# Fused attention and MLP block: weighted sums of two steps joined into one burst at 24 of 128 steps

## The chip, the cores and the metric

The kernel runs on one core of a Trainium2 chip. The metric is the device time in microseconds of one execution. It stood at 1092.6 us before the change (median of three runs, 1092.5 to 1093.32).

## The reference

The input x has 2048 tokens of width 448. The block adds three things: x itself, an attention and an MLP, both of the layer-normalized x.

```python
xn = layernorm(x)
q = (xn @ wq) in 16 heads of 28;  k = xn @ wk;  v = xn @ wv      # one k and v for all heads
p = softmax(q k^T * 28 ** -0.5);  o = p v
y = layernorm(xn)
out = x + o @ wo + gelu(y @ w1 + b1) @ w2 + b2                   # hidden width 1792
```

The layer norm has no weights. All is float32.

## The kernel before

**Stages.** The 2048 tokens lie as 16 tiles of 128, four tiles to a chunk of 512. Until about 475 us the kernel normalizes x, makes q, k and v, and runs the MLP. After that comes the attention stage, which this change touches; all its order is written out by hand, and each engine works through its own list in that order.

**Units and steps.** A *unit* is a chunk of 512 queries and a group of four heads: 16 units. A unit takes eight *steps*, each of two key tiles of 128: 128 steps, numbered n = 0 to 127, with n = 8u + i for step i of unit u. In units 1 to 15 (`TURNED`) three heads are computed in the step; the weights of the fourth head were computed earlier with queries on the partitions, stored in DRAM (`td`), and come back as `half` tiles, which VectorE transposes.

**What a step issues.** A string in `ORDERS` gives the order of a step, one letter an action; `ORDERS[u in TURNED][n % 2]` picks it.

- `s`: one score matmul of 128 keys x 512 queries (L871), and ScalarE's exp of it into half of a *pair* buffer (L872). Six a step, eight in unit 0.
- `m`: one matmul for the row maxima of later units (L521), and VectorE's maximum of it (L522). At most three in an even step and five in an odd one; a running quota stops them at step 117.
- `t`: one matmul of the fourth heads to come (L555), and VectorE's scaled copy with its maximum (L556); every fourth one ends a row block and frees two exps. In even steps, until the list is empty at step 94.
- `x`: one such exp over 1024 columns on ScalarE (L573), if one is free; each second one issues four stores to `td` on SP's queue.
- `T`: VectorE's transposition of the fourth head's weights for both key tiles of the step (L854), into one pair buffer.
- `n`: the next piece of a finished unit's normalization. `o`: the next piece of an output projection: 12 matmuls (L752 to L754) into one bank and VectorE's addition (L756), in four steps after every fourth unit, and with nine matmuls near the end. `e`: once a unit, the maxima of the next unit are set into its queries.
- `P`: the *burst*. `pv` multiplies the four heads' weights of one key tile by v, each head in its own 32 columns of the array, and adds into the bank `po` (L840); a float32 matmul is two records in the trace, so one key tile is eight records. The burst at the end of step n takes the two key tiles of step n - 1.

**Buffers.** PSUM has eight banks: one is `po`, and seven (`ring`) serve `s`, `m`, `t`, `e` and `o` alike. A matmul that needs a bank waits until an earlier user of one has been read by ScalarE or VectorE. There are `PAIRS` = 9 pair buffers; a step needs four of them (three for six scores, one for the transposition), each until `pv` has read both its halves. A `half` buffer holds four steps' worth of the fourth head; there are three. At the start of every step one part of the next unit's `half` is loaded; before the load VectorE writes one element of it (L723), which takes over the wait for the buffer.

Of the kernel before, what the change touches and what calls it, by code (L numbers as in the profile page):

```python
# [9 lines left out]
F32 = mybir.dt.float32  # L10
F32R = mybir.dt.float32r
# [5 lines left out]
P = 128  # L17
S, D, H, DH, F = 2048, 448, 16, 28, 1792
NT = S // P
CT = 4  # L20
NCH = NT // CT
CW = CT * P
NG = H // 4
NF = F // P
EPS = 1e-5
SCALE = DH ** -0.5
BURST = 2
PAIRS = 9
MLP_MAX = 18
ORDERS = (("nsmsmsnomssmstmssxmP", "nsmsmsemssmsomssnxmP"), ("nmsstTmsosnmssP", "nmsmssxmeosTmsnsmP"))  # L30
TURNED = tuple(range(1, 16))
RAWS = 2
GELU = 0.044715, 0.7978845608028654
LEAD = 11
NH = 8
HD = D // 2

# [2 lines left out]
def block_kernel(ctx, tc, x, wq, wk, wv, wo, w1, b1, w2, b2, out):  # L40
# [4 lines left out]
    def f(t):  # L45
        return t.bitcast(F32)
# [8 lines left out]
    def heads_of(u):  # L55
        return 3 if u in TURNED else 4
# [56 lines left out]
    def mtile(shape):  # L113
        return mp.tile(shape, F32, name="m")
# [97 lines left out]
    def bn_end(c, k0=0, n=CT):  # L212
        for k in range(k0, k0 + n):
            dve.bn_aggr(lnp[:, CT * c + k, :], sts[c][:, k, :])
        ts = slice(CT * c + k0, CT * c + k0 + n)
        r = rstd(lnr[:, ts], lnp[:, ts, 1], n)
        next(r)
        yield
        next(r)
        dve.scalar_tensor_tensor(lnb[:, ts], lnp[:, ts, 0], -1.0, lnr[:, ts], op0=ALU.mult, op1=ALU.mult)  # L220
        yield
# [9 lines left out]
    def norm_both():  # L231
        dve.tensor_mul(lnq, lnp[:, :, 1], lnr)
        dve.tensor_mul(lnq, lnq, lnr)
        r = rstd(lnq, lnq, NT)
        next(r)
        yield
        next(r)
        dve.tensor_mul(lnq, lnq, lnr)
        dve.scalar_tensor_tensor(lnqb, lnp[:, :, 0], -1.0, lnq, op0=ALU.mult, op1=ALU.mult)
        act.activation(warm, one, AF.Tanh)  # L240
        yield
# [61 lines left out]
    def norm_gen(c, bank):  # L303
        center, turn = norm_parts(c, True, False, bank)
        for k in range(CT + 1):
            if k > 0:
                turn(k - 1)
            yield
            if k < CT:
                center(k)  # L310
            yield
# [85 lines left out]
    def spin(n, t=None):  # L397
        for _ in range(n):
            pe.matmul(idle if t is None else t, ident, ident, start=True, stop=True)  # L399
# [9 lines left out]
    for c, at in ((2, ((0, 1), (0, 2), (0, 2), (0, 3))), (3, ((1, 0), (1, 1), (1, 2), (1, 3)))):  # L409
        for k in range(CT):  # L410
            later(*at[k], lambda t=CT * c + k: bn(t))
        g = bn_end(c)
        for k in range(2):
            later(c - 1, 0, lambda g=g: next(g), True)
    g = norm_both()
# [13 lines left out]
    qss, ots = {}, {}  # L429
# [16 lines left out]
    for c in range(NCH):  # L446
        center, turn = norm_parts((c + 1) % NCH, c + 1 == NCH, bank=lambda shape: (qbank, mtile)[next(turns) % 2](shape))
        for i in range(4):
# [7 lines left out]
            if i in ((2, 3) if c == 0 else (1, 3)):  # L456
                n = 2 * c + i // 3
# [216 lines left out]
    for c in range(1, NCH):  # L674
        g = norm_gen(c, lambda shape: php.tile(shape, F32, name="ph"))
# [4 lines left out]
    for n in range(len(mslots) + 2):  # L680
        c, ft = mslots[n] if n < len(mslots) else (NCH, n - len(mslots))
# [28 lines left out]
    att = ctx.enter_context(tc.tile_pool(name="att", bufs=2))  # L710
    mp = ctx.enter_context(tc.tile_pool(name="ring", bufs=7, space=PSUM))
    op = ctx.enter_context(tc.tile_pool(name="op", bufs=1, space=PSUM))

    wor = att.tile([P, NG, D], F32, name="wor", bufs=1)
    halves = {}

    def load_d(u, i):
        assert stored[u] == CT - 1
        h, r = divmod(i, 4)
        if r == 0:  # L720
            halves[u, h] = att.tile([P, 4 * CT, 256], F32, name="half", bufs=3)
        part = halves[u, h][32 * r:32 * r + 32]
        dve.memset(part[0:1, 0, 0:1], 0.0)  # L723
        nc.sync.dma_start(part, td[u][:, r, :, 256 * h:256 * h + 256])

    woh = att.tile([P, NG, D], F32R, name="woh", bufs=1)
    wol = att.tile([P, NG, D], F32R, name="wol", bufs=1)
    pool.memset(wor, 0.0)
# [4 lines left out]
    def prep_wo(g):  # L733
        act.activation(woh[:, g, :], wor[:, g, :], AF.Copy)
        pool.tensor_sub(wol[:, g, :], wor[:, g, :], f(woh[:, g, :]))
# [3 lines left out]
    def load_rows_of(c, tiles):  # L739
        for k in tiles:  # L740
            rows[c, k] = keep.tile([P, D], F32, name="a", bufs=4)
            dve.memset(rows[c, k][0:1, 0:1], 0.0)
            nc.sync.dma_start(rows[c, k], ad[:, CT * c + k, :])

    def o_jobs(c, gs, tiles=range(CT)):
        last = NG - 1 in gs
        for k in tiles:
            po = mtile([P, D])
            ts = slice(k * P, (k + 1) * P)
            for g in gs:  # L750
                oth, otl = ots[c, g]
                pe.matmul(po, oth[:, ts], woh[:, g, :], start=(g == gs[0]), stop=False)  # L752
                pe.matmul(po, oth[:, ts], wol[:, g, :], start=False, stop=False)  # L753
                pe.matmul(po, otl[:, ts], woh[:, g, :], start=False, stop=(g == gs[-1]))  # L754
            a = rows[c, k]
            dve.tensor_add(a, a, po)  # L756
            if last:
                (nc.scalar if k % 2 and c == NCH - 1 else nc.sync).dma_start(ov[:, CT * c + k, :], a)
            yield

    def o_tiles(c, g):
        ots[c, g] = [att.tile([P, CW], F32R, name=n, bufs=5) for n in ("oth", "otl")]
        return ots[c, g]

    def norm_jobs(u, po):
# [36 lines left out]
    def end_jobs(u, po):  # L802
        while side.step() or oside.step():
            pass
        c, g = units[u]
        oth, otl = o_tiles(c, g)
        jobs = o_jobs(c, [g])
        tr, rb, on = att.tile([P, CW], F32, name="tr2", bufs=1), att.tile([P, CW], F32, name="tr", bufs=1), att.tile([P, CW], F32, name="oc", bufs=1)
        rc = att.tile([P, CW // 32], F32, name="rc", bufs=1)
        last = mtile([P, P])  # L810
        spin(9, last)

        def blocks(t, h):
            return t[:, h].rearrange("p (a b) -> p a b", b=32)

        def shares(i):
            h, r = slice(256 * i, 256 * i + 256), slice(8 * i, 8 * i + 8)
            dve.transpose(tr[:, h], po[:, h])
            dve.reciprocal(rc[:, r], blocks(tr, h)[:, :, 0])
            dve.transpose(blocks(rb, h), rc[:, r, None].to_broadcast([P, 8, 32]))  # L820
            dve.tensor_mul(on[:, h], po[:, h], rb[:, h])
            act.activation(oth[:, h], on[:, h], AF.Copy)
            return lambda: dve.tensor_sub(otl[:, h], on[:, h], f(oth[:, h]))

        low = shares(0)
        low()
        low = shares(1)
        next(jobs)
        low()
        for _ in jobs:  # L830
            pass
# [20 lines left out]
    def turn_blocks(u, kt):  # L852
        p = pair_of()
        dve.transpose(p.rearrange("p k (g j) -> p g k j", j=32),  # L854
                      halves[u, kt // 8][:, :, 32 * (kt % 8):32 * (kt % 8) + 64].rearrange("p g (k j) -> p g k j", j=32))
        ps[u, kt, 3], ps[u, kt + 1, 3] = p[:, 0], p[:, 1]

    def pair_of():
        return att.tile([P, 2, CW], F32, name="p", bufs=PAIRS)

# [21 lines left out]
    steps = [(u, kt) for u in range(NU) for kt in range(0, NT, 2)]  # L882
    pvq = [(u, kt) for u in range(NU) for kt in range(NT)]
    total = 4 * CT * len(heads)
    left = total - maxed
    weight = [0 if n >= len(steps) - LEAD else (3, 5)[n % 2] + (u == 0) for n, (u, kt) in enumerate(steps)]
    for n, (u, kt) in enumerate(steps):
        if n == 0:
            loads = pool
        if n == len(steps) - 14:  # L890
            load_rows_of(NCH - 1, range(CT))
        if u + 1 < NU:
            load_d(u + 1, kt // 2)
        if 4 <= n < 4 + NG:
            prep_wo(n - 4)
        if u + 1 < NU and kt < 8:
            load_q(u + 1, (kt // 2,))
        jobs = [(u, kt + k, j) for k in range(2) for j in range(heads_of(u))]
        for what in ORDERS[u in TURNED][n % 2]:
            if what == "s":  # L900
                score(*jobs.pop(0))
            elif what == "m":
                if maxed < total - left + left * sum(weight[:n + 1]) / sum(weight):
                    maxed += mxs.step()
            elif what == "t":
                tq.step()
            elif what == "x":
                turned_exp()
            elif what == "T":
                if u in TURNED:  # L910
                    turn_blocks(u, kt)
            elif what == "e":
                if kt == (6 if u + 2 < NU else 10) and u + 1 < NU:
                    load_max(u + 1)
            elif what == "n":
                side.step()
            elif what == "o":
                if n == len(steps) - 5:
                    oside.add(o_jobs(NCH - 1, range(NG - 1)))
                oside.step()  # L920
            elif what == "P":
                assert not jobs
                for _ in range(BURST if n else 0):
                    pv(*pvq.pop(0))
    while pvq:
        pv(*pvq.pop(0))
# [27 lines left out]
```

## Time and profile before

| | |
|---|---|
| runs | 1092.6, 1092.5, 1093.32 us |
| profiled execution | 1092.67 us, of which 1090.9 us are the span from its first to its last instruction |
| granted TensorE clock | 0.999 |
| TensorE (PE) busy | 1079.5 us, 99% of the span |
| VectorE (DVE) busy | 910.4 us, 83% |
| ScalarE (ACT) busy | 736.4 us, 68% |
| GpSimd (POOL) busy | 562.5 us, 52% |

In rows of instruction groups the columns are line, engine, operation, output and inputs, shapes, count, then the busy time in us and the mean of one in ns, then the engine's idle time before them in us and what ended it. In rows of the timeline they are start in us, length in us, engine, line, operation, output and inputs, shape and count; a bracket holds the idle time before and what ended it. A row of the timeline can stand for several instructions in a row. In a row of a stretch of time they are its bounds, its length, then the busy time of PE, PEld (weight loads), DVE, ACT and POOL with the number of instructions, the granted clock, the share of the DMA engines and GB/s.

### The profile page before, as it was taken

To read this page: it belongs to the slowest core of one execution; us is meant where nothing else is said; L and a number is where in the kernel's file an instruction comes from. 1 tells how busy PE (TensorE), PEld (TensorE's weight loads), DVE (VectorE), ACT (ScalarE), POOL (GpSimd) and SP (SyncE) were. 2 spreads that over 40 slices of the span, in tenths; PEclk is the share of its full clock that TensorE was granted. 3 is DMA by queue.
4 is the path that set the end of the run, shared out by engine and by line. 5 is a ranking of instruction groups with operands and counts; after the bars stand their busy time and mean duration, and the time that the engine had idled before them with its cause. 6 is when DMAs were issued, how large, how long until landed. Compare 5 with 4: busy or idle time off the path is not lost.

```text
span 1090.9 us, 17542 instructions
## 1 busy us (share of the span) xinstructions
PE 1079.5 (99%) x5777; PEld 713.7 (65%) x5777; DVE 910.4 (83%) x1847; ACT 736.4 (68%) x1279; POOL 562.5 (52%) x694
## 2 busy tenths in 40 slices
PE   9999999999999999999999999999999999999998
PEld 8778888888888888865555556555556455555444
DVE  7789889888988998887898997899986889876744
ACT  6675565666666666559777776677775777765783
POOL 6359787778767877854343433433342343243220
PEclk9999999999999999999999999999999999999999
DMA  8774555777877777767977799588797778895720
GB/s 274 214 231 136 154 145 157 194 176 185 217 181 180 183 201 180 214 161 156 200 189 175 183 212 214 141 198 193 183 202 183 175 172 194 203 197 137 183 46 35
DMA packets 140512, 195.15 MB, mean 179 GB/s; under 512 B 17086, under 2 KB 96116, under 8 KB 140420
## 3 DMA queue, kind: packets, MB, share of 16 engines
q1 hardware_dynamic: 127684, 172.11, 63.0%
q0 software_dynamic: 11328, 21.33, 8.9%
q8 instruction: 46, 0.75, 0.3%
q10 hardware_dynamic: 1408, 0.57, 0.2%
q14 instruction: 46, 0.38, 0.1%
HBM read 115.22 MB, written 77.71 MB: 177 GB/s over the span
## 4 chain that ended last, share of the span: by engine, by line
PE 89%; ACT 3%; DVE 3%; DMA 2%; POOL 1%; issue 1%; SPq 0%; DVEq 0%; ACTq 0%; POOLq 0%
PE po L840 22%; PE m L521 17%; PE m L871 17%; PE m L633 10%; PE ph L180 9%; PE m L555 5%; PE qp L180 1%; DMA td<-raw 1%; PE m L752 1%; DVE mx L522 1%; PE m L753 1%; PE m L754 1%; PE ph L185 1%; PE ph L183 1%; ACT raw L573 1%; PE m L399 1%
## 5 line engine op out<-in xcount | busy, mean ns | idle before, releaser
L522 DVE TENSOR_REDUCE mx<-m 128x1 f32<-128x512 f32 x784 | 506.5, 680 | 81.1 <-PE m L521 72.3
L872 ACT ACTIVATE p<-m 128x512 f32<-128x512 f32 x784 | 402.6, 609 | 163.2 <-PE m L871 163.2
L521 PE MATMUL m<-ks,qm 128*128 128x512 f32 x784 | 322.1, 411 | 0.1
L871 PE MATMUL m<-xh,ks 128*128 128x512 f32 x784 | 258.6, 399 | 1.0 <-DVE half L723 1.0
L840 PE MATMUL po<-p,vs 128*32 128x512 f32 x2048 | 246.0, 598 | 0.0
L521 PEld LDWEIGHTS m<-ks,qm 128*128 128x128 f32 x784 | 147.0, 187 | 117.9 <-ACT p L872 34.5
L871 PEld LDWEIGHTS m<-xh,ks 128*128 128x128 f32 x784 | 144.2, 188 | 52.0 <-ACT p L872 15.0
L556 DVE TENSOR_SCALAR_CACHE_REDUCE raw<-m 128x512 f32<-128x512 f32 x240 | 161.1, 689 | 15.2 <-PE m L555 7.0
L854 DVE STREAM_TRANSPOSE p<-half 128x1024 f32<-128x1024 f32 x120 | 148.2, 1236 | 5.3 <-PE po L840 3.3
L573 ACT ACTIVATE raw<-raw,m 128x1024 f32<-128x1024 f32 x120 | 133.1, 1151 | 0.0
L840 PEld LDWEIGHTS po<-p,vs 128*32 128x32 f32 x2048 | 53.5, 109 | 120.1 <-issue 114.2
L603 ACT ACTIVATE hx<-ph,b1t 128x512 f32<-128x512 f32 x55 | 37.9, 690 | 131.9 <-PE ph L185 122.1
L555 PE MATMUL m<-ks,q 128*128 128x512 f32 x240 | 94.8, 395 | 1.1 <-DVE mx L522 0.6
L618 POOL TENSOR_TENSOR hl<-hx,hh 128x512 fp32r<-128x512 f32 x56 | 73.2, 1306 | 34.6 <-ACT hh L616 34.6
L633 PE MATMUL m<-w2h,hl 128*128 128x448 f32 x224 | 82.5, 370 | 0.3 <-POOL hl L618 0.3
L633 PE MATMUL m<-w2l,hh 128*128 128x448 f32 x224 | 81.4, 365 | 0.4 <-DVE w2l L346 0.4
L633 PE MATMUL m<-w2h,hh 128*128 128x448 f32 x224 | 81.4, 364 | 0.1
L611 POOL TENSOR_TENSOR hx<-hx,hz 128x512 f32<-128x512 f32 x56 | 73.1, 1306 | 4.7
L606 POOL TENSOR_TENSOR hz<-hz,hx 128x512 f32<-128x512 f32 x56 | 72.8, 1299 | 4.7
L508 POOL DMA_DIRECT2D xh<-mn x15 | 8.1, 543 | 124.3 <-ACT mn L504 124.3
L180 PE MATMUL ph<-xh,w1h 128*128 128x512 f32 x165 | 65.0, 394 | 0.0
L180 PE MATMUL ph<-xh,w1l 128*128 128x512 f32 x165 | 64.6, 391 | 0.0
(181 smaller groups left out, 1376.0 us busy)
## 6 DMA issues: line engine op xcount, KB each, us to landing
td<-raw SPq DMA_DIRECT2D x240, 256.0 KB
half<-td SPq DMA_DIRECT2D x120, 512.0 KB
xh<-qd POOLq DMA_DIRECT2D x60, 168.0 KB, 4.6
a<-in_A_x_dram SPq DMA_DIRECT2D x32, 224.0 KB
qm<-qd POOLq DMA_DIRECT2D x112, 56.0 KB, 4.4
qd<-qe SPq DMA_DIRECT2D x24, 256.0 KB
qm<-qd SPq DMA_DIRECT2D x84, 56.0 KB
ad<-a SPq DMA_DIRECT2D x16, 224.0 KB
```

The costliest lines, as they stand in the source:

```text
L180: pe.matmul(ps, w, v, start=(n == 0), stop=False)
L521: pe.matmul(pm, qm[:, t * P:(t + 1) * P], ks[:, n * CW:(n + 1) * CW], start=True, stop=True)
L522: dve.tensor_reduce(mx[:, CT * j + t, n:n + 1], pm, axis=AX.X, op=ALU.max)
L555: pe.matmul(sc, q3[i][:, t * P:(t + 1) * P], ks[:, n * CW:(n + 1) * CW], start=True, stop=True)
L556: dve.tensor_scalar(raw[:, :, 4 * n:4 * n + 4, :].rearrange("p r b i -> p b r i"), sc.rearrange("p (b r i) -> p b r i", r=4, i=32), SCALE, ...
L573: act.activation(raw[:, rs], raw[:, rs], AF.Exp, bias=m3[:, 4:5], scale=1.0)
L618: pool.tensor_sub(hl, hx, f(hh))
L633: pe.matmul(m2[k], h[:, k * P:(k + 1) * P], w[:, ft, :], start=(ft == 0 and i == 0), stop=(ft == NF - 1 and i == 2))
L840: pe.matmul(po[32 * j:32 * j + 32, :], vs[:, kt, :], ps.pop((u, kt, j)), start=(kt == 0), stop=(kt == NT - 1))
L854: dve.transpose(p.rearrange("p k (g j) -> p g k j", j=32), halves[u, kt // 8][:, :, 32 * (kt % 8):32 * (kt % 8) + 64].rearrange("p g (k j) ...
L871: pe.matmul(s, ks[:, kt * P:(kt + 1) * P], qss[u][:, j, :], start=True, stop=True)
L872: act.activation(p, s, AF.Exp, scale=SCALE)
```

## The change

- Steps in `JOINED` skip their burst, and the next step that does not skip makes up for it: its burst takes four key tiles instead of two. There are 24 such steps: 8u + 5 for units 1 to 13 (`QUIET`), and 41, 43, 73, 75, 105, 107 (steps with output projections), 117, 119, 121, 123 and 125 (after the last maxima).
- A quiet step and the step after it have an order of their own. The quiet step has four scores instead of six, four maxima instead of five, one `t`, and no `T` or `x`. The step after it has the eight scores left, four maxima instead of three, `x`, and both transpositions: the quiet step's before its last four matmuls, its own right before the burst. The even step had the `t` before, and the odd steps had the `x`.
- There are 12 pair buffers instead of 9. The room comes from three places: the raw output weights (`wor`) lie in the first `half` buffer; `oth` and `otl` (the normalized output of a unit, in two parts) have four buffers instead of five; a scratch tile of the last unit lies in a pair buffer.

```diff
-BURST = 2
-PAIRS = 9
+PAIRS = 12
 MLP_MAX = 18
-ORDERS = (("nsmsmsnomssmstmssxmP", "nsmsmsemssmsomssnxmP"), ("nmsstTmsosnmssP", "nmsmssxmeosTmsnsmP"))
+ORDERS = (("nsmsmsnomssmstmssxmP", "nsmsmsemssmsomssnxmP"), ("nmsstTmsosnmssP", "nmsmssxmeosTmsnsmP"),
+          ("nsmsomxsssnsTmssmTP", "nmsmesmotsnmsP"))
...
+QUIET = {8 * u + 5 for u in range(1, 14)}
+JOINED = QUIET | {41, 43, 73, 75, 105, 107, 117, 119, 121, 123, 125}
...
-    wor = att.tile([P, NG, D], F32, name="wor", bufs=1)
...
+    half = att.tile([P, 4 * CT, 256], F32, name="half", bufs=3)
+    wor = half.rearrange("p g c -> p (g c)")[:, 0:NG * D].rearrange("p (g n) -> p g n", g=NG)
...
-        ots[c, g] = [att.tile([P, CW], F32R, name=n, bufs=5) for n in ("oth", "otl")]
+        ots[c, g] = [att.tile([P, CW], F32R, name=n, bufs=4) for n in ("oth", "otl")]
...
-        tr, rb, on = att.tile([P, CW], F32, name="tr2", bufs=1), att.tile([P, CW], F32, name="tr", bufs=1), att.tile([P, CW], F32, name="oc", bufs=1)
+        tr, rb, on = pair_of()[:, 0], att.tile([P, CW], F32, name="tr", bufs=1), att.tile([P, CW], F32, name="oc", bufs=1)
...
+    jobs, turnq = [], []
...
-        jobs = [(u, kt + k, j) for k in range(2) for j in range(heads_of(u))]
-        for what in ORDERS[u in TURNED][n % 2]:
+        jobs.extend((u, kt + k, j) for k in range(2) for j in range(heads_of(u)))
+        if u in TURNED:
+            turnq.append((u, kt))
+        for what in ORDERS[2 if {n, n - 1} & QUIET else u in TURNED][n % 2]:
...
             elif what == "T":
-                if u in TURNED:
-                    turn_blocks(u, kt)
+                if turnq:
+                    turn_blocks(*turnq.pop(0))
...
             elif what == "P":
-                assert not jobs
-                for _ in range(BURST if n else 0):
+                assert n in QUIET or not jobs and not turnq
+                while n not in JOINED and len(steps) * 2 - len(pvq) < 2 * n:
                     pv(*pvq.pop(0))
```

## The prediction

> **What bounds the kernel now.** I read the profile's page first, then the waits of TensorE and the busy time by stretch, then the timeline of two steps in the attention stage, and last the timeline of its end.
>
> ```profile
> PE 1079.5 (99%) x5777; PEld 713.7 (65%) x5777; DVE 910.4 (83%) x1847; ACT 736.4 (68%) x1279; POOL 562.5 (52%) x694
> PE 89%; ACT 3%; DVE 3%; DMA 2%; POOL 1%; issue 1%; SPq 0%; DVEq 0%; ACTq 0%; POOLq 0%
> L840 PE MATMUL po<-p,vs 128*32 128x512 f32 x2048 | 246.0, 598 | 0.0
> ```
>
> TensorE is the bound and 89% of the chain. The change touches the attention stage alone, from about 484 us on, and there TensorE never rests at full clock, while VectorE has 117 us and ScalarE 167 us to spare over the stage:
>
> ```profile
> 484.00:1080.00 596.00, 596.00 (x3511) 312.34 (x3503) 479.24 (x874) 428.79 (x828) 207.99 (x334) 1.00 0.75 173
> ```
>
> So every nanosecond of TensorE's own time saved is gained, and every wait that TensorE gets is lost. The timeline of one burst, with what the readers do around it:
>
> ```profile
> 701.59 1.89 DVE L522 TENSOR_REDUCE mx<-m 128x1 f32<-128x512 f32 x3 [0.39 <-PE m L521]
> ...
> 703.28 1.16 ACT L573 ACTIVATE raw<-raw,m 128x1024 f32<-128x1024 f32 x1
> 703.54 0.42 PE L521 MATMUL m<-ks,qm 128*128 128x512 f32 x1
> 703.89 1.92 PE L840 MATMUL po<-p,vs 128*32 128x512 f32 x16
> 704.32 1.58 ACT L872 ACTIVATE p<-m 128x512 f32<-128x512 f32 x3
> 705.75 0.50 PE L521 MATMUL m<-ks,qm 128*128 128x512 f32 x1
> 705.75 0.06 DVE L723 MEMSET half<- 1x1 f32 x1
> 706.09 0.62 PE L871 MATMUL m<-xh,ks 128*128 128x512 f32 x2
> 706.29 0.69 DVE L522 TENSOR_REDUCE mx<-m 128x1 f32<-128x512 f32 x1 [0.48 <-PE m L521]
> 706.52 3.05 ACT L872 ACTIVATE p<-m 128x512 f32<-128x512 f32 x6 [0.62 <-PE m L871]
> 706.55 0.40 PE L555 MATMUL m<-ks,q 128*128 128x512 f32 x1
> 706.78 0.39 PE L521 MATMUL m<-ks,qm 128*128 128x512 f32 x1
> 706.98 0.69 DVE L556 TENSOR_SCALAR_CACHE_REDUCE raw<-m 128x512 f32<-128x512 f32 x1
> 707.01 0.66 PE L871 MATMUL m<-xh,ks 128*128 128x512 f32 x2
> 707.51 0.40 PE L521 MATMUL m<-ks,qm 128*128 128x512 f32 x1
> 707.60 1.24 DVE L854 STREAM_TRANSPOSE p<-half 128x1024 f32<-128x1024 f32 x1
> 708.32 1.92 PE L840 MATMUL po<-p,vs 128*32 128x512 f32 x16
> 708.76 1.25 DVE L522 TENSOR_REDUCE mx<-m 128x1 f32<-128x512 f32 x2
> ...
> 710.17 0.50 PE L521 MATMUL m<-ks,qm 128*128 128x512 f32 x1
> ```
>
> What to see: ordinary matmuls start every 0.23 us (706.55, 706.78, 707.01), but the burst starts 0.35 after the one before it, and after it the first two stand 0.34 apart. While TensorE is in the burst, the readers work off what is left: the exps begun at 704.32 and the reductions begun at 708.76 in the next burst. From these rows I take the prices of the readers. An exp follows the last by 0.48 (three in 1.58, six in 3.05, one being about 0.61), an exp of the stored kind (L573) holds ScalarE 1.04 (703.28 to 704.32), a reduction 0.60 (three in 1.89, one being 0.69), the pass of L556 0.62 (706.98 to 707.60), a transposition 1.16 (707.60 to 708.76). An idle ScalarE starts 0.43 after its matmul (706.09 to 706.52), VectorE 0.54 after the first of a step (705.75 to 706.29).
>
> **What is saved.** At the very end two bursts stand together today:
>
> ```profile
> 1076.61 3.64 PE L840 MATMUL po<-p,vs 128*32 128x512 f32 x32
> ...
> 1080.18 2.27 PE L399 MATMUL m<-ident 128*128 128x128 f32 x18
> ```
>
> Four key tiles in one burst take 1080.18 - 1076.61 = 3.57, two take 705.75 - 703.89 = 1.86 (or 710.17 - 708.32 = 1.85 from the next). One burst instead of two saves 2 x 1.86 - 3.57 = 0.15, one entry (0.35 - 0.23 = 0.12) and one spacing after it (0.34 - 0.23 = 0.11). With the spread of these rows that is 0.31 to 0.38; I take 0.35. The change skips the burst at 24 steps (13 in QUIET, 11 more in JOINED), so 24 x 0.35 = 8.4 us are saved if nothing else moves. The Trainium skill (TensorEngine Tiling (Array Packing), Key Properties) says that changing the tiling mode, not just the tile, drains TensorE; the trace agrees with 0.35 per burst, and by that rule alone the time would be 1084.3.
>
> **What is paid.** The scores and maxima share seven PSUM banks. A matmul can start only when one of the seven has been read. Today the burst of 1.86 us after each step lets the readers catch up; without it they don't. A full bank does stop TensorE in this trace, in the first steps:
>
> ```profile
> 480.85 1.19 ACT L872 ACTIVATE p<-m 128x512 f32<-128x512 f32 x2
> ...
> 481.32 0.71 ACT L872 ACTIVATE p<-m 128x512 f32<-128x512 f32 x1
> 481.60 0.50 PE L871 MATMUL m<-xh,ks 128*128 128x512 f32 x1
> 481.93 0.40 PE L521 MATMUL m<-ks,qm 128*128 128x512 f32 x1
> ```
>
> The exp begun at 480.85, 0.70 long like its neighbour, ends at 481.55, and the matmul that waited starts 0.05 later; its successor starts 0.33 later instead of 0.23. So a bank is free 0.66 after an exp starts (0.61 + 0.05) and 0.73 after a reduction starts.
>
> (a) *The quiet pairs of units 1 to 11.* Counting from the first matmul after a burst, TensorE would start its matmuls at 0, 0.34 and every 0.23 after that; the 21st and last (12 scores, 8 maxima, one of L555) at 0.34 + 19 x 0.23 = 4.71. In the new order the pass of L555 moves one step forward, into the quiet step; every fourth of these frees an L573, so that one falls between the 13th and 14th matmul of the pair, where ScalarE is already behind. ScalarE: the scores numbered 2, 4, 7, 9, 10 and 12 get their exps at 0.77, 1.26, 1.92, 2.40, 2.88, 3.36; then L573 from 3.84 to 4.88; then the next exp. Banks free at 1.43, 1.92, 2.58, 3.06, 3.54, 4.02, and the seventh only at 5.54. VectorE: reductions and L556 start at 0.54, 1.14, 1.74, 2.34, 2.96, 3.56, 4.16, banks free at 1.27 to 4.89; then the transposition holds it until 5.9. The 21st matmul needs 14 of the first 20 banks back. Thirteen are back by 4.89, the fourteenth at 5.54. It waits 5.54 - 4.71 = 0.83. Add 0.05, half of the wider spacing after a wait. Net 0.88 - 0.35 = +0.53 a pair, 11 pairs: +5.8. Nothing gives this back, since the joined burst that follows is TensorE's own time. Bounds a pair: -0.35 if no bank is ever short, +0.7 if banks return 0.1 later than I take.
>
> (b) *The quiet pairs of units 12 and 13.* L555 and L573 have run out. The last matmul is the 20th, at 4.48, and needs 13 banks: ScalarE has given seven and VectorE six by 4.3. No wait: 2 x -0.35 = -0.7.
>
> (c) *Six pairs at the output projections* (41, 43, 73, 75, 105, 107):
>
> ```profile
> 668.59 0.62 DVE L756 TENSOR_TENSOR a<-a,m 128x448 f32<-128x448 f32 x1 [1.70 <-PE m L754]
> 669.12 1.24 DVE L854 STREAM_TRANSPOSE p<-half 128x1024 f32<-128x1024 f32 x1
> 669.29 0.39 PE L521 MATMUL m<-ks,qm 128*128 128x512 f32 x1
> 669.61 1.92 PE L840 MATMUL po<-p,vs 128*32 128x512 f32 x16
> 670.29 1.25 DVE L522 TENSOR_REDUCE mx<-m 128x1 f32<-128x512 f32 x2
> ```
>
> The projection's twelve matmuls give the readers time (VectorE is idle for 1.70), but then the addition and the transposition stand before two reductions whose banks come back at 671.0 and 671.6, and the burst at 669.61 that covered this is gone. TensorE goes on after 669.29 with six matmuls; the last of them, at 669.29 + 6 x 0.23 = 670.67, finds all seven banks taken and waits for an exp until 670.9. Wait 0.2, saving 0.35, sum -0.12 a pair, -0.7 in all. If instead each matmul must take the bank used seven before it, the fourth, at 670.23, waits for 671.0 and the pair loses 0.42: +2.5. If there is no wait, -2.1.
>
> (d) *Five pairs at the end* (117 to 126), with scores alone:
>
> ```profile
> 1036.78 1.66 PE L871 MATMUL m<-xh,ks 128*128 128x512 f32 x6
> 1037.31 3.05 ACT L872 ACTIVATE p<-m 128x512 f32<-128x512 f32 x6 [0.43 <-PE m L871]
> ```
>
> Twelve scores in a row: the twelfth, at 0.34 + 10 x 0.23 = 2.64, needs the fifth bank back, and that exp starts at 0.43 + 4 x 0.48 = 2.35, bank free at 3.0. Wait 0.36: no gain at 117, 119 and 121. The other two (123 and 125) hold nine such projection matmuls as in (c) in each step, twelve of which left VectorE 1.70 idle; nine give ScalarE more than the 0.36 that it lacks, and these pairs gain 0.35 each. Sum -0.7; bounds -1.75 and +0.5.
>
> *The rest costs nothing while its cover holds.* Twelve pair buffers are three steps of four, just what a joined burst needs; TensorE's full stretch above shows that nine cost nothing. Both transpositions now stand late in the even step: the first ends near 6.1 of its pair, and the third key tile of the burst, which reads it, starts near 5.9 + 1.7 = 7.6; behind it on VectorE stand only reductions, counted above. Without that cover a burst would wait up to 1.2. The stores that L573 issues on SP move by one step, against loads issued a whole unit ahead; the loads on POOL's queue that L555's stream issues move likewise. Output weights now lie in the first half buffer: its next user is the 1x1 write of step 8, and the last reader is long done:
>
> ```profile
> 511.92 1.15 POOL L735 TENSOR_TENSOR wol<-wor,woh 128x448 fp32r<-128x448 f32 x1 [3.16 <-ACT woh L734]
> ...
> 515.45 0.06 DVE L723 MEMSET half<- 1x1 f32 x1
> ```
>
> Cover 515.45 - 513.07 = 2.4 us; gone, VectorE and then TensorE would wait by what is missing, once. Four buffers for oth/otl suffice, since a chunk's projections end four steps before the next chunk writes; tr2 in a pair buffer is free at the end.
>
> Sum, against the profiled execution's own 1092.67 (span 1090.9 and 1.8 around it; the median of the runs is 1092.6): 5.8 - 0.7 - 0.7 - 0.7 = +3.7, that is **1096.4**. The Trainium skill (TensorEngine Tiling (Array Packing), PSUM Bottleneck) says that tiling speeds up TensorE but not the emptying of PSUM, which may become the bottleneck; today's trace does not show that after 484 us, and the sum says that the change brings it about.
>
> **The rivals.** *As the change means it*: the banks come back in time and 24 bursts are saved: 1092.67 - 8.4 = 1084.3. For it: 117 us of idle VectorE. Against it: the idle time lies in and after the bursts, not before them. It decides if the wait of a quiet pair stays near nothing; at 0.35 a pair only breaks even. *L573 does not delay the pair* (its exp falls in another step, or the scores behind it are not short): then the fourteenth bank is VectorE's at 4.89, the wait 0.18, the pair -0.17, and the sum 11 x -0.17 - 2.1 = -4.0: 1088.7. For it: it is one instruction. Against it: the order puts it there in every unit while there are any. *Banks in strict rotation*: (c) turns to +2.5 and the joined scores wait more often: 3.7 + 3.2, and if the other 16 pairs lose 0.1 each by it, 1.6 more: 1101.2. *The bursts don't join, or gains and waits balance*: 1092.7; the loop does skip them, so this is mere chance.
>
> **How the numbers follow.** Forecast 0.62, of which a tenth or so is so mild that it lies below 1094.8; strict rotation 0.12; L573 harmless 0.10; as meant 0.13; balance 0.03. About 0.2%, 2.2 us, is what a measurement can tell from no change here. Faster: 0.10 + 0.13 = 0.23. Same: 0.03 + 0.08 = 0.11. Slower: 0.66. The forecast's own range is 1093.5 to 1099.5 from the bounds of (a) and (c). The range given reaches from the harmless L573, 1088.5, to strict rotation with a little more, 1101.5; it leaves out the case as meant and the far ends.
>
> **What would show it.** Right: 103 bursts, 25 of them of 32 records or more, each about 3.57 long; TensorE waits, now absent, of 0.5 to 0.9 in each even step after a quiet one, ended by ScalarE (L872) late and by VectorE (L522) before it, and hardly any in units 12 and 13; shorter pairs at 123 and 125. Wrong: no new waits of TensorE after 484 us, or waits before L840 for a transposition instead.

## The result, and the profile after

The changed kernel takes **1103.93 us** (median of four runs, 1103.62 to 1104.12) against 1092.55; the ratio is 1.0102, with a 95% interval of 1.0089 to 1.0114. It is 11.4 us slower. The direction was forecast; the size was forecast at 3.7 us, and the result lies 2.4 us above the top of the range. The profiled execution took 1104.02 us, and its span is 1102.2.

In the rows of after, the lines stand two or three higher: the maxima (`m`) are L523, their reductions L524, the `t` matmul L557 and its pass L558, the stored exp (`x`) L575, the bursts L843, the transpositions L857, the scores (`s`) L874 and their exps L875. First the page of after: the busy times, the chain that ended last, and the bursts.

```profile
PE 1085.4 (98%) x5777; PEld 715.8 (65%) x5777; DVE 908.1 (82%) x1847; ACT 735.9 (67%) x1279; POOL 561.2 (51%) x694
PE 89%; ACT 4%; DVE 4%; DMA 1%; issue 1%; POOL 1%; DVEq 0%; ACTq 0%; POOLq 0%; SPq 0%
L843 PE MATMUL po<-p,vs 128*32 128x512 f32 x2048 | 241.1, 597 | 0.0
```

The records of the bursts fell from 246.0 to 241.1 us, so the joining happened: the trace has 78 bursts of 16 records and 25 of 32 or more, 103 in all. But ScalarE and VectorE took one per cent more of the chain each. The attention stage by its stretch of time (columns as in the prediction), and then the waits of TensorE in it (engine, line, what it waited for; us in total, number, longest):

```profile
484.00:1090.00 606.00, 600.08 (x3499) 313.42 (x3495) 477.65 (x875) 428.27 (x829) 207.19 (x334) 1.00 0.76 171
```

```profile
PE m L874 <- ACT p L875: 4.5, 13, 0.4
PE m L523 <- ACT p L875: 1.4, 2, 0.7
```

TensorE, never idle in this stage before, is idle for 5.92 of 606 us, all of it a matmul that waits for an exp (L875): 13 waits of at most 0.4, and two of 0.7. That is only half of the 11.3 us by which the span grew. The rest is hidden in busy time. Around a wait the rows of matmuls read up to 0.50 instead of 0.39, so two starts that stand up to half a microsecond apart, instead of 0.23, leave no idle time between the rows. For such waits the *starts* of the rows must be compared, not the idle columns.

So I compared the two traces pair by pair, by the start of the first matmul after the burst that ends the pair. For the pair of unit 2 the rows are, of before and of after:

```profile
574.59 0.50 PE L521 MATMUL m<-ks,qm 128*128 128x512 f32 x1
...
583.59 0.50 PE L521 MATMUL m<-ks,qm 128*128 128x512 f32 x1
```

```profile
575.55 0.50 PE L523 MATMUL m<-ks,qm 128*128 128x512 f32 x1
...
578.49 1.09 ACT L875 ACTIVATE p<-m 128x512 f32<-128x512 f32 x2
579.45 1.17 ACT L575 ACTIVATE raw<-raw,m 128x1024 f32<-128x1024 f32 x1
579.52 1.29 DVE L524 TENSOR_REDUCE mx<-m 128x1 f32<-128x512 f32 x2
579.97 0.40 PE L523 MATMUL m<-ks,qm 128*128 128x512 f32 x1
580.27 0.49 PE L874 MATMUL m<-xh,ks 128*128 128x512 f32 x1
580.49 3.06 ACT L875 ACTIVATE p<-m 128x512 f32<-128x512 f32 x6
580.73 1.23 DVE L857 STREAM_TRANSPOSE p<-half 128x1024 f32<-128x1024 f32 x1
581.15 0.50 PE L874 MATMUL m<-xh,ks 128*128 128x512 f32 x1 [0.39 <-ACT p L875]
581.49 0.40 PE L523 MATMUL m<-ks,qm 128*128 128x512 f32 x1
581.82 3.64 PE L843 MATMUL po<-p,vs 128*32 128x512 f32 x32
...
585.39 0.50 PE L523 MATMUL m<-ks,qm 128*128 128x512 f32 x1
```

The pair took 9.00 us and now takes 9.84. What to see: the stored exp (L575) holds ScalarE from 579.45 to 580.49, the next exp ends 0.61 later, at 581.10, and 0.05 after that the second last matmul of the pair starts, 0.88 after the one before it. The joined burst is 585.39 - 581.82 = 3.57 long, as forecast. The differences of all pairs, worked out in this way:

| pairs | forecast, each | measured, each | measured, sum |
|---|---|---|---|
| quiet, units 1-4, 6-8, 10, 11 | +0.53 | +0.79 to +0.84 | +7.3 |
| quiet, units 5 and 9 (45/46, 77/78) | +0.53 | +2.36 and +2.35 | +4.7 |
| quiet, units 12 and 13 | -0.35 | -0.18 and -0.26 | -0.4 |
| six at the projections | -0.12 | -0.01 to +0.03 | +0.1 |
| 117, 119, 121 | 0 | +0.23, +0.33, +0.42 | +1.0 |
| 123, 125 | -0.35 | -0.36 and -0.34 | -0.7 |
| everything else | 0 | | -0.6 |

The last line is what is left to the 11.3 us by which the last burst ends later. Two of the pairs stand out. The timeline of after around step 45:

```profile
696.36 0.39 PE L523 MATMUL m<-ks,qm 128*128 128x512 f32 x1
696.74 0.50 PE L557 MATMUL m<-ks,q 128*128 128x512 f32 x1
697.23 0.49 PE L874 MATMUL m<-xh,ks 128*128 128x512 f32 x1
...
697.76 0.60 ACT L875 ACTIVATE p<-m 128x512 f32<-128x512 f32 x1 [0.58 <-PE m L874]
...
698.41 0.50 PE L523 MATMUL m<-ks,qm 128*128 128x512 f32 x1 [0.69 <-ACT p L875]
698.75 0.62 PE L874 MATMUL m<-xh,ks 128*128 128x512 f32 x2
```

The pair began at 695.33, after a joined burst in which the readers had emptied everything. ScalarE idles for 0.58 before the exp at 697.76: nothing is full. Yet the maximum at 698.41 starts 1.18 after the score before it, 0.05 after the exp of that very score ended (697.76 + 0.60). It waited for the bank of its direct predecessor. The list of banks in the built program says the same: the bank a matmul writes is not chosen on the chip when one comes free, but was assigned to the instruction when the program was put together. In before, the attention matmuls take banks that were last used 4 to 10 uses ago (a projection's matmuls count as one use); in after, 1 to 13. The distance of one occurs twice, at a maximum in each of the pairs at 45 and 77. The maximum at 698.41 is the first of them, while by the trace two other banks had been read since 692.15 and 692.76.

### The profile page after: what moved, and what is told of

It reads as the page before. It is cut to its first block, busy times and chain, and to the rows that moved or that the text cites. A ratio compares the mean times of both kernels' runs of the same rounds, so it can differ in the third digit from the quotient of the medians.

```text
span 1102.2 us, 17495 instructions
## 1 busy us (share of the span) xinstructions
PE 1085.4 (98%) x5777; PEld 715.8 (65%) x5777; DVE 908.1 (82%) x1847; ACT 735.9 (67%) x1279; POOL 561.2 (51%) x694
## 4 chain that ended last, share of the span: by engine, by line
PE 89%; ACT 4%; DVE 4%; DMA 1%; issue 1%; POOL 1%; DVEq 0%; ACTq 0%; POOLq 0%; SPq 0%
PE po L843 21%; PE m L523 17%; PE m L874 16%; PE m L635 11%; PE ph L182 10%; PE m L557 5%; ACT p L875 1%; ACT raw L575 1%; PE m L755 1%; PE m L756 1%; DVE mx L524 1%; PE m L757 1%; PE ph L187 1%; PE ph L185 1%; PE m L401 1%
## 5 line engine op out<-in xcount | busy, mean ns | idle before, releaser
L524 DVE TENSOR_REDUCE mx<-m 128x1 f32<-128x512 f32 x784 | 506.5, 680 | 97.4 <-PE m L523 87.7
L875 ACT ACTIVATE p<-m 128x512 f32<-128x512 f32 x784 | 402.1, 612 | 175.2 <-PE m L874 173.4
L523 PE MATMUL m<-ks,qm 128*128 128x512 f32 x784 | 319.8, 409 | 1.4 <-ACT p L875 1.4
L874 PE MATMUL m<-xh,ks 128*128 128x512 f32 x784 | 266.2, 405 | 5.5 <-ACT p L875 4.5
L843 PE MATMUL po<-p,vs 128*32 128x512 f32 x2048 | 241.1, 597 | 0.0
L523 PEld LDWEIGHTS m<-ks,qm 128*128 128x128 f32 x784 | 147.1, 188 | 104.1 <-ACT p L875 31.7
L874 PEld LDWEIGHTS m<-xh,ks 128*128 128x128 f32 x784 | 144.4, 188 | 67.9 <-ACT p L875 29.7
L558 DVE TENSOR_SCALAR_CACHE_REDUCE raw<-m 128x512 f32<-128x512 f32 x240 | 160.6, 688 | 15.0 <-PE m L557 6.9
L857 DVE STREAM_TRANSPOSE p<-half 128x1024 f32<-128x1024 f32 x120 | 147.9, 1234 | 3.0 <-PE po L843 2.9
L843 PEld LDWEIGHTS po<-p,vs 128*32 128x32 f32 x2048 | 56.0, 109 | 126.9 <-issue 121.6
L575 ACT ACTIVATE raw<-raw,m 128x1024 f32<-128x1024 f32 x120 | 132.9, 1150 | 0.0
L557 PE MATMUL m<-ks,q 128*128 128x512 f32 x240 | 95.0, 396 | 0.7 <-DVE mx L524 0.5
```

The costliest lines, as they stand in the source:

```text
L523: pe.matmul(pm, qm[:, t * P:(t + 1) * P], ks[:, n * CW:(n + 1) * CW], start=True, stop=True)
L524: dve.tensor_reduce(mx[:, CT * j + t, n:n + 1], pm, axis=AX.X, op=ALU.max)
L557: pe.matmul(sc, q3[i][:, t * P:(t + 1) * P], ks[:, n * CW:(n + 1) * CW], start=True, stop=True)
L558: dve.tensor_scalar(raw[:, :, 4 * n:4 * n + 4, :].rearrange("p r b i -> p b r i"), sc.rearrange("p (b r i) -> p b r i", r=4, i=32), SCALE, ...
L575: act.activation(raw[:, rs], raw[:, rs], AF.Exp, bias=m3[:, 4:5], scale=1.0)
L843: pe.matmul(po[32 * j:32 * j + 32, :], vs[:, kt, :], ps.pop((u, kt, j)), start=(kt == 0), stop=(kt == NT - 1))
```

## The experiments

The theory after this result: two causes, the stored exp (`x`, L575) standing before the seventh exp, as forecast, and banks that were assigned in a bad order, which the prediction did not have. The rivals: the pairs at 45 and 77 lose because they follow joined bursts at the projections; the buffers or the other joined bursts cost something.

**The stored exp left out of the order after a quiet step.** It is done by a later `x`.

```diff
-          ("nsmsomxsssnsTmssmTP", "nmsmesmotsnmsP"))
+          ("nsmsomsssnsTmssmTP", "nmsmesmotsnmsP"))
```

> The changed kernel, but the step after a quiet one has no place for the stored exp (L573 of the kernel before); it falls into the next odd step, where it was before the change. All work is still done. Theory A (ScalarE's 1.04 us stands before the last scores of the joined pair, and the banks, which are fixed when the program is built, are worst there): the eleven pairs that cost +0.80 each fall to between -0.35 and +0.2, the 2.35 at steps 45 and 77 falls too, and the time is 1091 to 1095. Theory B (VectorE is short: two transpositions late and eight reductions in a row): taking work from ScalarE changes little, the pairs still cost +0.5 or more, and the time stays above 1099.

Measured: 1093.82 us (1093.57 to 1095.16), ratio 1.0009 [1.0, 1.0018]. Seven of the nine ordinary quiet pairs end within 0.1 of before, those of units 4 and 8 at +0.27 and +0.29, and those of 45 and 77 at +0.47 and +0.45. The same pair of unit 2, timeline:

```profile
575.04 6.19 ACT L875 ACTIVATE p<-m 128x512 f32<-128x512 f32 x12 [1.37 <-PE m L874]
...
578.68 0.40 PE L523 MATMUL m<-ks,qm 128*128 128x512 f32 x1
578.91 0.66 PE L874 MATMUL m<-xh,ks 128*128 128x512 f32 x2
579.41 0.42 PE L523 MATMUL m<-ks,qm 128*128 128x512 f32 x1
579.76 3.64 PE L843 MATMUL po<-p,vs 128*32 128x512 f32 x32
```

Twelve exps now run in one stretch, and the last matmuls follow each other by 0.23 to 0.27. So taking out one letter, an instruction of 1.04 us on an engine that is two thirds busy, takes away ten of the eleven microseconds. But it also gave new bank assignments everywhere, with none at a distance below four, so this run alone does not separate the two causes.

**The banks named by hand.** The order of after is kept; a table names the bank of each of the 1335 uses, always the one that is read first by my replay, that is, by the readers' ends worked out with the row prices of the prediction.

```diff
-    mp = ctx.enter_context(tc.tile_pool(name="ring", bufs=7, space=PSUM))
+    mp = ctx.enter_context(tc.tile_pool(name="ring", bufs=1, space=PSUM))
+    banks = iter(BANKS)
+    def mtile(shape):
+        return mp.tile(shape, F32, name=f"m{next(banks)}")
...
-        s = mp.tile([P, CW], F32, name="m")
+        s = mtile([P, CW])
```

> The changed kernel with its order untouched, but each matmul's PSUM bank is named by a table: always the bank whose last reader, by the row prices of the prediction, is done first. Theory A1 (the banks that the build chose make a good part of the waits): the 2.35 at steps 45 and 77 falls to the level of the other units, these from +0.80 to about +0.3 to +0.5, and the time is 1095.5 to 1098. Theory A2 (the banks don't matter, the pair is short of readers whatever the bank): the time stays within 1 us of 1103.9, and 45 and 77 keep their 2.35.

Measured: 1098.24 us (1097.9 to 1099.06), ratio 1.0052 [1.0037, 1.0067]: 5.7 us faster than after, by nothing but the choice of banks. The quiet pairs of units 1 to 11 all end +0.51 to +0.61, those of 45 and 77 among them; units 12 and 13 end at -0.03 and -0.60, and the end is as in after. The timeline at step 45 and the waits of TensorE (in kernels with named banks the maxima are L539, their reductions L540, the `t` matmuls L573, the scores L895, their exps L896, the bursts L864):

```profile
695.63 0.39 PE L573 MATMUL m<-ks,q 128*128 128x512 f32 x1
695.86 0.39 PE L895 MATMUL m<-xh,ks 128*128 128x512 f32 x1
696.09 0.39 PE L539 MATMUL m<-ks,qm 128*128 128x512 f32 x1
```

```profile
PE m L539 <- DMA qm<-qd: 0.7, 1, 0.7
```

The same maximum that waited 1.18 starts 0.23 after its predecessor, and none of the fifteen waits for an exp is left as idle time. What remains is one wait of 0.7 for queries that a DMA brings, in the first step of unit 13. So the bank assignment costs 1.84 in each of the pairs at 45 and 77 and about 0.2 in each of the nine others: 2 x 1.84 + 9 x 0.21 = 5.6.

What the pair of unit 2 still waits for, in the same run:

```profile
575.25 0.50 PE L539 MATMUL m<-ks,qm 128*128 128x512 f32 x1
...
579.21 1.29 DVE L540 TENSOR_REDUCE mx<-m 128x1 f32<-128x512 f32 x2
579.96 1.10 PE L895 MATMUL m<-xh,ks 128*128 128x512 f32 x2
580.19 3.06 ACT L896 ACTIVATE p<-m 128x512 f32<-128x512 f32 x6
580.89 0.46 PE L539 MATMUL m<-ks,qm 128*128 128x512 f32 x1
```

The second of the two reductions at 579.21 ends at 580.50, 5.25 after the pair began, and 0.06 later the second last matmul starts (580.56, the second in the row at 579.96). The last one follows at 580.89, after the exp behind the stored exp, which ends about 580.80. Both readers hold the pair up now, VectorE first.

**Only the quiet pairs joined.**

```diff
-JOINED = QUIET | {41, 43, 73, 75, 105, 107, 117, 119, 121, 123, 125}
+JOINED = QUIET
```

> The changed kernel with JOINED = QUIET: the 13 quiet pairs stay joined, the other eleven joins (projection steps and the end) are undone. If the 2.35 at 45 and 77 comes from the joined projection steps right before them, units 5 and 9 fall to +0.80 and the time is about 1100.5. If it comes from the bank that the build gives the maximum after the third score there, it may stay, and the time is 1103.5 to 1104. The end loses its +0.28 either way.

Measured: 1104.8 us (1103.86 to 1105.08), ratio 1.0109 [1.0093, 1.0126]. The ordinary pairs lose 0.79 to 0.83, those of 45 and 77 lose 2.37 and 2.38. The joined bursts before them are gone and the loss stays, as do the two assignments at a distance of one in the list of banks, so the rival falls.

**Only the other eleven joined.**

```diff
-QUIET = {8 * u + 5 for u in range(1, 14)}
+QUIET = set()
```

> The changed kernel with QUIET empty: only the eleven joins at the projection steps and at the end are left, in the old order of the steps, with all buffers as in the changed kernel. From the changed kernel's own trace the six projection pairs gave 0.0 each and the end +0.28, so the time is 1092.5 to 1093; if the buffers (weights in the half buffer, twelve pairs, four oth/otl) cost anything, it shows here as more. The prediction had -0.7 - 0.7, that is 1091.2.

Measured: 1093.57 us (1092.8 to 1094.06), ratio 1.0005 [0.9996, 1.0014]. The projection pairs end between -0.01 and +0.03, the five at the end +0.24, +0.33, +0.41, -0.34, -0.34, as in after. Twelve pair buffers, and the room made for them, cost nothing that shows.

**Both causes taken away**: banks by hand and no `x` in the order after a quiet step (the same two edits, with a table worked out for this order).

> Both cures together: banks by a table as in the second experiment, and no place for L573 in the joined pair as in the first; the joins are those of the change. If the two causes are all that the quiet pairs suffer from, each of the thirteen gains between 0.1 and 0.35, the projection pairs 0.0 to -0.1 each and the end +0.3, and the time is 1089 to 1091. If VectorE's transpositions also hold them up, the pairs stay at +0.2 or more and the time above 1094.

Measured: 1093.54 us (1093.06 to 1094.5), ratio 1.0006 [0.9997, 1.0015]. It missed: the quiet pairs of units 1 to 11 still lose 0.08 to 0.20 instead of gaining. With the banks named in both, the stored exp is worth 1098.24 - 1093.54 = 4.7 us, not ten. The timeline of VectorE and two matmuls in the pair of unit 2 (the pass of `t` is L574 here, the reductions L540):

```profile
577.49 0.68 DVE L574 TENSOR_SCALAR_CACHE_REDUCE raw<-m 128x512 f32<-128x512 f32 x1
578.09 0.08 DVE L574 DVE_READ_ACCUMULATOR raw<-m 128x1 f32 x1
578.21 0.16 DVE L580 TENSOR_REDUCE m<-m 128x1 f32<-128x4 f32 x1
578.28 0.68 DVE L540 TENSOR_REDUCE mx<-m 128x1 f32<-128x512 f32 x1
579.02 0.06 DVE L745 MEMSET half<- 1x1 f32 x1
579.11 1.29 DVE L540 TENSOR_REDUCE mx<-m 128x1 f32<-128x512 f32 x2
...
579.36 0.40 PE L539 MATMUL m<-ks,qm 128*128 128x512 f32 x1
579.86 0.73 PE L895 MATMUL m<-xh,ks 128*128 128x512 f32 x2
```

The score at 579.86 starts 0.50 after its predecessor. Its bank comes from the first of the two reductions at 579.11, which ends about 579.80. VectorE is now the late reader, through instructions that the prediction had counted at nothing or not seen: between the pass and the next reduction stand an accumulator read and a maximum over four columns, so that the two starts are 0.79 apart instead of 0.62; around the write of one element two reductions start 0.83 apart instead of 0.60. So 0.17 and 0.23 us go to items whose own rows read 0.06 to 0.16. The Trainium skill (VectorE: DVE Perf Modes, The TRN2 errata) says that VectorE's operations with a source in SBUF pay a fixed extra latency per instruction, which weighs the less the larger the operand. The trace agrees in kind with the 0.17, of which the maximum over four columns, read from SBUF, is a part; the write of one element has no source, and its 0.23 stands by this trace alone.

**The order of before with banks by hand.**

> The kernel before, in its own order and with its own buffers, with only the banks named by a table. Its trace has hardly any waits of TensorE after 484 us, so at most about 0.6 us can go (the first steps, and 0.2 to 0.3 in each of steps 109 and 110): 1092 to 1092.9. If the banks of the build cost the kernel before much, as they did the changed one, it would fall below 1091.

Measured: 1090.69 us (1090.25 to 1091.38), ratio 0.9981 [0.9971, 0.999]: faster by 2 us where at most about 0.6 was expected. The differences by step are small, the largest at unit 13's steps 109 to 111 (-0.32, -0.29, -0.11). From the first burst to the last they add up to 1.9 us, so before lost a little to its banks too.

**Other steps joined**, without `x`: the odd steps of units where all stood ready by my replay, first with the banks as assigned, then with banks by hand.

```diff
-QUIET = {8 * u + 5 for u in range(1, 14)}
-JOINED = QUIET | {41, 43, 73, 75, 105, 107, 117, 119, 121, 123, 125}
+QUIET = {9, 13, 21, 25, 37, 41, 53, 61, 69, 73, 85, 93, 97, 101, 105, 109, 113}
+JOINED = QUIET | {44, 76, 122, 124, 126}
```

> Joins at other steps, with the banks of the build: quiet pairs at 9, 13, 21, 25, 37, 41, 53, 61, 69, 73, 85, 93, 97, 101, 105, 109 and 113, without a place for L573, and plain joins at 44, 76, 122, 124 and 126, each chosen so that by the row prices, with the bank that is free first, the pair waits little. 22 bursts fewer, worth 7.4. If the banks of the build still cost waits of 0.2 to 0.5 in each pair, most of that is eaten and the time is 1091.5 to 1093.5; if banks don't matter here, 1086 to 1088.

> The same joins as in the seventh experiment, with the banks named by a table. If waits for banks are what stands between a joined burst and its 0.34, this gains about 5 to 6 us on the kernel before: 1086 to 1088.5. If something else takes it (late transpositions, pair buffers), TensorE waits at L840's successor or for a transposition, and the time is above 1090.

Measured: 1094.78 us (1094.26 to 1095.26), ratio 1.0016 [1.0007, 1.0026], and with banks by hand 1091.17 us (1090.57 to 1091.89), ratio 0.9984 [0.9975, 0.9993]. The first lies above both of its forecasts, the second above 1090, where its rival put it. The 3.6 us between them are banks alone. In the second, the pairs that begin at 41, 44, 73, 76, 105 and 109 gain 0.37 to 0.61, 101 gains 0.14, 124 and 126 gain 0.36 each; the ordinary units' pairs lose up to 0.19, as in the run with both causes taken away, and 122 loses 0.58.

**Only the joins that gained**, with banks by hand and without `x`.

```diff
-QUIET = {8 * u + 5 for u in range(1, 14)}
-JOINED = QUIET | {41, 43, 73, 75, 105, 107, 117, 119, 121, 123, 125}
+QUIET = {41, 73, 101, 105, 109}
+JOINED = QUIET | {44, 76, 124, 126}
```

> The order of before with every matmul's bank named by the table, and only nine joined bursts, at the pairs of steps 41, 44, 73, 76, 101, 105, 109, 124 and 126; the units 1 to 4, 6 to 8, 10 and 11 keep two bursts a pair. Theory that a joined burst saves its 0.33 us wherever no matmul of the pair waits for a bank, and costs only through such waits: each of these nine ends 0.15 to 0.6 earlier than in before, some 3 us in all, and the rest is the 1090.7 of the order of before with named banks: 1087 to 1088.5. Rival, that a joined burst's saving is eaten by the next wait of VectorE or ScalarE in the same unit, so that the ends of later pairs drift back: 1090 to 1091.

Measured: **1088.49 us** (1088.3 to 1089.13) against 1093.11 of before, run beside it, ratio 0.9962 [0.9948, 0.9975]. It beats both kernels and lies at the edge of what the first theory expected. The pairs at 41, 44, 73, 76, 105, 109, 124 and 126 end 0.34 to 0.61 earlier than in before and later pairs keep it, so the rival falls; 101 misses, with -0.02. But not all of this is the joins' doing. In the order of before with banks by hand the pair at 109 ends 0.61 earlier too, without a joined burst, so joining it gains nothing. Against that run seven joins are worth 0.31 to 0.41 each, and 101 and 109 nothing. The page and the attention stage:

```profile
PE 1074.9 (99%) x5777; PEld 719.2 (66%) x5777; DVE 909.5 (84%) x1847; ACT 735.2 (68%) x1279; POOL 561.0 (52%) x694
...
L864 PE MATMUL po<-p,vs 128*32 128x512 f32 x2048 | 244.2, 598 | 0.0
```

```profile
484.00:1076.00 592.00, 592.00 (x3509) 317.65 (x3502) 479.13 (x875) 427.51 (x828) 207.42 (x334) 1.00 0.76 175
```

TensorE is busy through the whole stage again, and the bursts' records are 1.8 us below before's 246.0: nine joined bursts instead of 24, of which seven pay.

## Why the prediction was right or wrong

**What is saved: right.** A joined burst takes 3.57, there are 25 of 32 records or more, and where nothing waits a pair gains 0.34 to 0.36 (123 and 125). All 24 savings are there; they are more than eaten.

**(a) The quiet pairs of units 1 to 11: the stored exp right, the choice of banks wrong, and this is the step that failed.** The stored exp does stand before the seventh exp, and without it the pairs are nearly even. But the step said that a matmul "can start only when one of the seven has been read", any one, as the description of the buffers ahead of it does, while each matmul waits for its own assigned bank. With banks assigned about in the order in which they are read, which comes nearest to the prediction's own model, the pair costs 0.51 to 0.61, against +0.53 forecast. Part of that agreement is luck. ScalarE was priced right: the exp behind the stored exp ends 5.55 after the pair began, so that its bank is free at 5.60, against 5.54 forecast. VectorE was not: its last bank before the transposition comes at 5.30, against 4.89. That holds the second last matmul until 5.31, and the last one, 0.34 behind it, starts about when the exp would have let it anyway. With the banks of after it costs 0.79 to 0.84, and 2.36 where a maximum was given the bank of the score right before it. Sum +12.0 instead of +5.8: 6.2 of the 7.6 us that the forecast lacks, and 5.6 of these 6.2 come from the banks. The prediction had a rival with a fixed assignment, "banks in strict rotation", but at a distance of always seven, which neither list of banks shows, and its 1101.2 still lies 2.7 short.

**(b) Units 12 and 13: near in size, "no wait" wrong for unit 13.** There is no `x`, and the pairs gain 0.18 and 0.26 (0.35 forecast), with a further 0.11 in the step after unit 13's. But in unit 13's pair two matmuls start 0.41 and 0.39 after the one before them, with 0.34 behind each, as two do in before (0.42 and 0.41). These waits nearly cancel in the difference; that they do was not foreseen.

**(c) The projection pairs: the mechanism right, too small by 0.12 each.** The rows of after at the pair that begins at 41:

```profile
673.53 0.39 PE L557 MATMUL m<-ks,q 128*128 128x512 f32 x1
673.77 0.49 PE L523 MATMUL m<-ks,qm 128*128 128x512 f32 x1
674.26 0.50 PE L874 MATMUL m<-xh,ks 128*128 128x512 f32 x1
674.60 0.36 PE L755 MATMUL m<-woh,oth 128*128 128x448 f32 x1
```

The score at 674.26 starts 0.49 after its predecessor and the next matmul 0.34 after it, against 0.23 each: a loss of 0.26 + 0.11 = 0.37 against the 0.34 saved. The forecast had the 0.2 of the wait, and left out the wider spacing behind it, which (a) had allowed for.

**(d) The end: the step mis-sized by 1.0 us.** 123 and 125 gain 0.35 each as forecast. 117, 119 and 121 were to break even and lose 0.33 on the mean. The pair that begins at 119, in after:

```profile
1051.50 3.71 PE L874 MATMUL m<-xh,ks 128*128 128x512 f32 x12
...
1052.10 5.99 ACT L875 ACTIVATE p<-m 128x512 f32<-128x512 f32 x12 [1.29 <-PE m L874]
1055.14 3.64 PE L843 MATMUL po<-p,vs 128*32 128x512 f32 x32
```

The first exp starts 0.60 after the first matmul of a pair, not the 0.43 that I had read from a bracket of idle time (the 0.53 between the two starts of that very row would have been nearer): the first matmul after a burst is itself 0.50 long. The fifth bank is then free at 0.60 + 4 x 0.49 + 0.66 = 3.22 instead of 3.0, and the twelve scores take 1055.14 - 1051.50 = 3.64, where 0.34 + 10 x 0.23 + 0.35 = 2.99 is what they take without a wait. The wait is 0.65, not 0.36; less the 0.34 saved, +0.31.

**The rest at nothing: right.** No burst waits for a transposition, the buffers cost nothing, and the first units stay within 0.2 of before.

**The other rivals.** "L573 does not delay the pair" is refuted by the timeline and by the run without it. "As the change means it" would need the banks back in time; the run with both causes taken away shows that even then VectorE's small instructions keep the pairs from gaining.

What stays open: a table that always takes the bank read first is not best everywhere. With `x` gone, seven ordinary pairs lost under 0.1 with the program's own banks and 0.14 to 0.20 with mine, probably because my replay's prices for VectorE were too low; a table with better prices was not run. Nor was a kernel with the seven joins that pay alone.

## What to carry to other kernels

When several readers empty a shared ring of PSUM buffers, ask which buffer each matmul was assigned, not how many are free: here two assignments at a distance of one cost 1.8 us each, and naming the banks alone gave 5.7 us in after and 2 in before. Look for lost time in the spacing of starts, since here a spacing of up to half a microsecond instead of 0.23 lengthened rows instead of showing as idle. And before taking away a long instruction of the bound engine that looks like mere overhead, list the readers that catch up behind it, with their one long instruction and all their small ones: join only where the trace shows that they are done.

## What was new of the hardware

A bank can be written again 0.05 us after the row of its reader ends; the rows above show it twice (581.10 to 581.15, 698.36 to 698.41). Tiny VectorE instructions (rows of 0.06 to 0.16 us) moved the next reduction by 0.17 to 0.23 us. And a stage whose main engine is idle for only 5.9 us had lost 11.3.
